# One attention and two-layer MLP kernel: GpSimd makes V's low part, and its planner gets new numbers

## The chip, the cores and the metric

The kernel runs on 1 core of a Trainium2 chip. The metric is the device time of one execution in microseconds; less is better.

## The reference

Attention with a threshold, then two gated MLP layers, all in float32:

```python
scores = (q @ k.T) / sqrt(64)                       # 4 batches, 8 heads, 576 rows, 64 columns
scores = where(scores >= max(scores, -1) - tau, scores, -1e9)
attn = exp(scores - max(scores, -1));  attn /= sum(attn) + 1e-9
x = attn @ v                                        # to 2304 rows of 512
h = x @ w_in                                        # 512 -> 2048
x = (h * tanh(softplus(h))) @ w_out                 # layer 1: Mish
h = x @ w2_in
out = (h * clip(h + 3, 0, 6) / 6) @ w2_out          # layer 2: hard swish
```

## The kernel before, in words

Precision is kept by splitting: each operand of a large matmul becomes a float16 high part and a float16 low part (the rest), and three products are summed. The low part of V, `vl`, is V times a scale `vs`, less its high part `vh`; the pv matmul adds both parts.

The weights come as 64-bit words and are turned into float32 by integer steps (`one_conversion`, L912): maximum (L785), scale, expansion on ScalarE (L921), a shift by three or a product by eight in two halves (c2: L929 on GpSimd, L931 on VectorE), two merges on VectorE (L937, L942). The first layer's weights (w1i, w1o) are then split in two (L961, L729); the second layer's go through a Strassen-like scheme with seven products (`combined`, L972), as does y between the layers (`split_sums`, L1100).

There are four stages. (1) Attention: for each of the 16 head pairs and each of 4 full query tiles and a tail tile of 64 rows, scores go to one of two PSUM buffers (`s`), VectorE takes the row maximum (`pk`, L1858), ScalarE the exponential (`ex`, L1868) and the threshold (`th`, L1863), VectorE the mask (`mk`, e_ex L1871), ScalarE the float16 high part (`ph`, L1876), GpSimd the low part (`pl`, L729 p_ph), a DMA transposes (`tr`), and PE multiplies with V (`pv`, L1897). (2) Woven into it, the first gemm of layer 1 for blocks of 256 rows whose attention is done (`inner`, L1260). (3) Layer 1's second gemm (`first_layer`, L1304), beside the conversion of w2i and w2o. (4) Layer 2, block by block (`second_layer`, L1381).

No order is written out by hand. Everything is a task with one or more engines, a duration for each (`{"dve": 0.88}`), buffers it holds, and a due time. `Plan.run` (L631) plays the tasks through a clock of each engine: again and again it takes for each engine the best candidate by due time among those that could start within a window (WINDOW, NEAR_LATE) and issues the one that starts first. This happens when the program is built; on the chip each engine works off its own list in order and waits on semaphores. So a duration in the code changes only the order, and, where a task names several engines (WHO, SHIFT, TAKE), who does it. A VectorE candidate for such a task is put back by SLOW in that comparison. The kinds in PORT are not planned beside GpSimd's.

Due times in the attention are START plus multiples of STEP; each task's own is shifted by NUDGE[name], and by EASE per kind. `V`'s loads and maxima are planned in `batch_values` (L1702), K's scaling, `vh` and `vl` in `pair` (L1748):

Of the kernel before, what the change touches and what calls it, by code (L numbers as in the profile page):

```python
# [52 lines left out]
PREP_AHEAD = 5.76
CONV_STEP = 1
CONV_AT = 5.423
LATE_STEP = 3.76
OUT_STEP = 2.681
OUT_AT = 149.789
V_AHEAD = 4.749
# [2167 lines left out]
```

## Time and profile before

| | us |
|---|---|
| median of 3 runs | 986.13 (984.49 to 987.72) |
| the profiled execution | 984.73 |
| its span, first to last instruction | 982.9 |
| PE busy | 922.2 (94%) |
| DVE busy | 797.9 (81%) |
| ACT busy | 650.8 (66%) |
| POOL busy | 409.2 (42%) |

PE is TensorE, DVE VectorE, ACT ScalarE, POOL GpSimd, SP SyncE, which issues the DMAs. The shares are means over stages with different limits, so they are to be read by stretches of the span.

### The profile page before, as it was taken

Reading aid. Unit: us, or ns where it says so; the run is one execution under the profiler, and the core shown is the slowest. Engines: PE = TensorE matmul, PEld = TensorE weight load, DVE = VectorE, ACT = ScalarE, POOL = GpSimd, SP = SyncE. Lnnn points to the kernel's source line nnn. Section 1 sums busy time; section 2 is a strip of 40 time slices with the busy share of each in tenths; the row PEclk is TensorE's granted clock in tenths of the full one; section 3 lists DMA queues with packets and bytes.
Section 4 is the critical chain, followed back from the end, with each engine's and each line's share of the span. In section 5 each row is a group of like instructions: output and inputs, shape, how many; then the busy total and the mean of one; then the engine's idle time right before and its main releaser. Section 6 shows DMA issues by size and latency. Waiting matters only on the chain.

```text
span 982.9 us, 25896 instructions
## 1 busy us (share of the span) xinstructions
PE 922.2 (94%) x10776; PEld 797.2 (81%) x10776; DVE 797.9 (81%) x1516; ACT 650.8 (66%) x1051; POOL 409.2 (42%) x354
## 2 busy tenths in 40 slices
PE   3669779999999999999999999999999999999996
PEld 1447457777777778888888888899999999999986
DVE  6998898888878888569999889888758758758864
ACT  6678688888888877567866778655444444545541
POOL 2777776766655667315656777720000000000000
PEclk9769789999999999999999999999999999999999
DMA  9899999999999999864654757750110110110001
GB/s 313 179 233 234 228 226 218 251 253 217 238 217 270 216 220 238 234 239 173 239 211 176 282 188 287 246 219 9 60 47 16 60 41 22 60 32 31 23 15 31
DMA packets 201798, 164.48 MB, mean 167 GB/s; under 512 B 174160, under 2 KB 174928, under 8 KB 195280
## 3 DMA queue, kind: packets, MB, share of 16 engines
q1 hardware_dynamic: 201680, 162.82, 61.1%
q8 instruction: 85, 1.39, 0.6%
q14 instruction: 33, 0.27, 0.1%
HBM read 84.28 MB, written 36.04 MB: 122 GB/s over the span
## 4 chain that ended last, share of the span: by engine, by line
PE 76%; DVE 13%; POOL 3%; DMA 3%; issue 2%; ACT 1%; SPq 0%; DVEq 0%; POOLq 0%; ACTq 0%
PE h_g L1241 15%; PE y_y L1356 13%; PE s_s L1849 7%; PE aux_pv L1897 5%; PE hp_g1a L1430 5%; PE h_g0a L1430 5%; PE hp_g1d L1430 2%; PE h_g0d L1430 2%; DMA pt_tr<-p_ph 2%; DVE e_ex L1871 2%; DVE nm_pk L1858 1%; POOL p_ph L729 1%; DVE top L785 1%; PE h_g1b L1430 1%; DVE gs_h L1336 1%
## 5 line engine op out<-in xcount | busy, mean ns | idle before, releaser
L729 POOL TENSOR_TENSOR p_ph<-e_ex,p_ph 128x128 f16<-128x128 f32 (+3 forms) x160 | 192.5, 1225 | 106.4 <-issue 54.8
L1583 PEld LDWEIGHTS <-gs_h 128*128 128x128 f16 x1512 | 146.8, 98 | 18.0 <-issue 1.5
L1430 PEld LDWEIGHTS <-w__h 128*128 128x128 f16 x2016 | 156.0, 98 | 1.2 <-issue 0.6
L1871 DVE SCALAR_TENSOR_TENSOR e_ex<-s_s,thr_th,e_ex 128x576 f32<-128x576 f32 x144 | 111.9, 812 | 15.3 <-ACT thr_th L1863 11.8
L1858 DVE TENSOR_REDUCE nm_pk<-s_s 128x1 f32<-128x576 f32 x144 | 104.6, 751 | 18.0 <-PE s_s L1849 17.0
L1868 ACT ACTIVATE e_ex<-s_s,nm_pk 128x576 f32<-128x576 f32 x144 | 104.1, 730 | 18.5 <-DVE nm_pk L1858 13.9
L1849 PE MATMUL s_s<-kd_lk,qs_qp 64*128 64x288 f32 x440 | 80.8, 480 | 36.4 <-DVE e_ex L1871 25.6
L1876 ACT ACTIVATE p_ph<-e_ex 128x576 f16<-128x576 f32 x144 | 94.8, 678 | 13.5 <-DVE e_ex L1871 9.1
L1430 PEld LDWEIGHTS <-w__u 128*128 128x128 f16 x1008 | 98.6, 98 | 0.0
L1897 PEld LDWEIGHTS <-pt_tr 128*128 128x128 f16 x2016 | 81.3, 103 | 11.1 <-issue 5.8
L1849 PEld LDWEIGHTS s_s<-kd_lk,qs_qp 64*128 64x128 f32 x440 | 41.4, 204 | 59.0 <-issue 39.5
L1897 PE MATMUL aux_pv<-vh,pt_tr 128*128 128x65 f16 (+1 forms) x1296 | 86.1, 203 | 1.9 <-DMA pt_tr<-p_ph 1.9
L729 DVE TENSOR_TENSOR gs_h<-g_ab,gs_h 128x896 f16<-128x896 f32 x72 | 74.6, 1087 | 15.9 <-ACT gs_h L1533 15.9
L1533 ACT ACTIVATE gs_h<-g_ab 128x1792 f16<-128x1792 f32 x36 | 59.6, 1690 | 27.4 <-DVE g_ab L729 27.4
L1897 PE MATMUL aux_pv<-vl_vl,pt_tr 128*128 128x64 f16 x720 | 70.7, 203 | 0.0
L1517 ACT ACTIVATE g_ab<-g_ab,aux,hscales 128x512 f32<-128x512 f32 x72 | 54.1, 804 | 16.9 <-DVE g_ab L1458 16.9
L1327 ACT ACTIVATE hp_e<-hl_l 128x512 f32<-128x512 f32 x72 | 42.4, 594 | 23.5 <-DVE gs_h L1336 23.2
L1290 ACT ACTIVATE he_t<-h_g,hin 128x512 f32<-128x512 f32 x63 | 42.9, 683 | 19.0 <-PE h_g L1241 15.1
L1523 DVE SCALAR_TENSOR_TENSOR g_ab<-g_ab,f 128x512 f32<-128x512 f32 x72 | 51.2, 747 | 5.0 <-ACT g_ab L1517 5.0
L1336 DVE SCALAR_TENSOR_TENSOR gs_h<-hp_e,fscales,gs_h 128x512 f16<-128x512 f32 x72 | 53.0, 743 | 2.1 <-ACT gs_h L1330 2.1
L1330 ACT ACTIVATE gs_h<-hp_e,fscales 128x512 f16<-128x512 f32 x72 | 47.3, 678 | 7.6 <-PE y_y L1356 6.8
L1448 ACT ACTIVATE s_ka<-h_g0a 128x512 f32<-128x512 f32 x27 | 16.1, 595 | 48.1 <-PE h_g0a L1430 47.9
(672 smaller groups left out, 2559.2 us busy)
## 6 DMA issues: line engine op xcount, KB each, us to landing
hd<-he_t SPq DMA_DIRECT2D x36, 512.0 KB, 4.2
hl_l<-hd SPq DMA_DIRECT2D x18, 1024.0 KB, 5.7
raw_lr<-in_moe_w_in SPq DMA_DIRECT2D x16, 1024.0 KB, 6.0
raw_lr<-in_moe_w_out SPq DMA_DIRECT2D x16, 1024.0 KB, 7.5
yd<-yl_zhy SPq DMA_DIRECT2D x9, 896.0 KB, 3.8
qs_qp<-in_q SPq DMA_DIRECT2D x10, 576.0 KB, 5.8
v_lv<-in_v SPq DMA_DIRECT2D x16, 320.0 KB, 4.7
kd_lk<-in_k SPq DMA_DIRECT2D x15, 288.0 KB, 3.9
```

The lines of the kernel that those rows point to most:

```text
L729: engine[e].tensor_tensor(dst, a, b, ALU.subtract)
L1241: mm(hv[:, j, :], wj[:, wl, c * P : (c + 1) * P], x.tile[:, c, xl, :], start=j == 0 and n == 0, stop=j == 1 and n == 11, skip_group_check= ...
L1336: nc.vector.scalar_tensor_tensor(s.tile[:, k, 1], g.tile.rearrange("p (a n) -> p a n", a=2), fs[:, fp : fp + 1], s.tile[:, k, 0], ALU.mult ...
L1356: mm(yv[:, h, :], wt[1][f // 2].tile[:, f % 2, wl, c * P : (c + 1) * P], gs[fp // COL].tile[:, fp % COL, gl, f % 2, :], start=fp == 0 and ...
L1430: mm(dst.tile[:, i * Q : (i + 1) * Q], wt[2][fp][wl].tile[:, right - 1, c * P : (c + 1) * P], x[xl].tile[:, c, left - 1], start=first and ...
L1583: mm(region(p), part[:, gl, left - 1], wt[3][fp][wl].tile[:, right - 1], start=fp == n == 0 and spot(p)[1] == 0, stop=fp == NG - 1 and n == 2,
L1849: mm(s[j].tile[:, half, :HALF], lh[r], rh[r], start=m == 0, stop=m == len(terms) - 1,)
L1858: nc.vector.tensor_reduce(neg.tile[:, j : j + 1], sv(j), AX.XY, ALU.max, negate=True)
L1868: nc.scalar.activation(ev(j), sv(j), AF.Exp, bias=neg.tile[:, j : j + 1])
L1871: nc.vector.scalar_tensor_tensor(ev(j), sv(j), thr.tile[:, j : j + 1], ev(j), ALU.is_ge, ALU.mult)
L1876: nc.scalar.activation(p16.tile[:, js, :S], e_.tile[:, js], AF.Copy)
L1897: mm(ov[:, dst, :d], pt.tile[:, j, ch, :], part.tile[:, src, vc, :], start=i == j == ch == 0 and part is vh, stop=j == w - 1 and ch == 8, ...
```

## The change

V's low part leaves VectorE. In `pair` both ways of making it are already there, and WHO["vl"] decides: before, one instruction `v_lo` on VectorE (scale and subtract); after, two on GpSimd, `v_scaled` (V times `vs`, in place) and `v_rest` (less `vh`), the second after the first, both due when the pair begins. Other entries of WHO let c2 of w2i's and w2o's conversions, their sums and low parts, y's low part and K's scaling go to other engines.

The planner's clock for VectorE, ScalarE and GpSimd now lets an instruction begin a little before the one ahead of it ends (OVERLAP), some thirty durations are new, and the constants and shifts (STEP, START, NUDGE and others) are new throughout: 2149 shifts stand where 1595 stood, 594 of these with the same value. No other operation is added or removed.

```diff
-STEP = 2.791
-START = 12
+STEP = 2.764
+START = 10.202
...
-V_FIRST = -0.435
+V_FIRST = 0.446
...
-SHIFT = {"pool": 1.0, "dve": 0.6}
+SHIFT = {"pool": 1.05, "dve": 0.43}
...
-SLOW = 0.413
+SLOW = 0.499
 WHO = {
-    "c20": ("dve",), "c21": ("pool",), "c30": ("pool", "dve"), "c31": ("pool", "dve"),
-    "q2": ("pool",), "q3": ("pool", "dve"), "u20": ("dve",), "u21": ("pool",),
-    "u30": ("pool",), "u31": ("pool", "dve"), "uy0": ("pool", "dve"), "uy1": ("dve",),
-    "kh": ("act",), "vh": ("act",), "vl": ("dve",), "q": ("dve",), "o0": ("dve",), "o1": ("dve",),
+    "c20": ("pool", "dve"), "c21": ("dve",), "c30": ("dve",), "c31": ("dve",),
+    "q2": ("pool", "dve"), "q3": ("pool", "dve"), "u20": ("pool",), "u21": ("pool", "dve"),
+    "u30": ("pool",), "u31": ("pool",), "uy0": ("dve",), "uy1": ("pool",),
+    "kh": ("pool", "act"), "vh": ("act",), "vl": ("pool", "dve"), "q": ("dve",), "o0": ("dve",), "o1": ("dve",),
 }
...
+OVERLAP = {"dve": 0.08, "act": 0.1, "pool": 0.04}
 NUDGE = {
...
             end = start + cost
-            self.clock[e] = end
+            self.clock[e] = max(start, end - OVERLAP.get(e, 0.0))
...
-        return task({"dve": 1.3}, top, [loaded], [raw], "zw" + name)
+        return task({"dve": 1.212}, top, [loaded], [raw], "zw" + name)
...
-        a = task({"dve": 1.28}, c3, b, [raw, t], "c" + nm)
-        a = task({"dve": 1.28}, c4, [a], [raw, t], "c" + nm)
+        a = task({"dve": 1.22}, c3, b, [raw, t], "c" + nm)
+        a = task({"dve": 1.22}, c4, [a], [raw, t], "c" + nm)
...
-                a = go({"act": 0.69}, relu, done, [g], f"r{fp}")
+                a = go({"act": 0.803}, relu, done, [g], f"r{fp}")
...
-                cost = {"dve": 0.17 + size / 960.0, "pool": 0.1 + size / 450.0}
+                cost = {"dve": 0.17 + size / 960.0, "pool": 0.2 + size / 490.0}
```

## Rows read from the trace of the kernel before

**Rows 1.** Page, head: span, PE's busy us (share) and instructions, granted clock in tenths.
```profile
span 982.9 us, 25896 instructions
...
PE 922.2 (94%) x10776; PEld 797.2 (81%) x10776; DVE 797.9 (81%) x1516; ACT 650.8 (66%) x1051; POOL 409.2 (42%) x354
...
PEclk9769789999999999999999999999999999999999
```

**Rows 2.** Stretch, length; busy us: PE, PEld, DVE, ACT, POOL; clock, DMA share, GB/s.
```profile
0.00:13.00 13.00, 2.66 (x8) 1.09 (x9) 6.28 (x15) 4.65 (x8) 1.52 (x16) 1.00 0.80 277
13.00:30.00 17.00, 10.50 (x71) 6.29 (x72) 15.79 (x34) 14.96 (x28) 7.90 (x7) 1.00 1.07 316
30.00:100.00 70.00, 52.51 (x557) 39.24 (x553) 65.29 (x137) 52.94 (x92) 54.18 (x50) 0.78 0.89 211
100.00:140.50 40.50, 27.93 (x266) 19.07 (x268) 34.56 (x79) 29.42 (x54) 27.16 (x25) 0.79 1.02 240
140.50:412.00 271.50, 269.23 (x3280) 213.52 (x3278) 230.82 (x427) 219.22 (x409) 174.16 (x157) 1.00 1.04 229
412.00:642.00 230.00, 227.73 (x2116) 203.94 (x2114) 201.11 (x344) 168.16 (x250) 142.20 (x101) 1.00 0.63 230
642.00:973.00 331.00, 329.30 (x4470) 312.28 (x4470) 240.99 (x480) 160.95 (x214) 2.12 (x2) 1.00 0.14 47
```

**Rows 3.** Waits of PE before 140.5 us: total us, times, longest us.
```profile
PE s_s L1849 <- DVE e_ex L1871: 27.8, 12, 4.7
```

**Rows 4.** Chain that ended last, 940 to 983 us: start us, us, what.
```profile
973.36 0.48 ACT out_v L1623
```

**Rows 5.** DVE's busy time of V's low part (L1799) alone, by stretches.
```profile
13.00:30.00 17.00, 2.55 (x3) 1.00 1.07 316
30.00:100.00 70.00, 1.36 (x1) 0.78 0.89 211
100.00:140.50 40.50, 0.97 (x2) 0.79 1.02 240
```

**Rows 6.** Chain that ended last, 0 to 32 us.
```profile
18.30 1.59 DVE vl_vl L1799 x2
...
23.22 2.30 PE s_s L1849 x8
```

**Rows 7.** POOL by form, whole run: operation, shape, count | busy us, mean ns | idle before.
```profile
L729 POOL TENSOR_TENSOR p_ph<-e_ex,p_ph 128x1024 f16<-128x1024 f32 x64 | 137.4, 2147 | 0.0
...
L729 POOL TENSOR_TENSOR p_ph<-e_ex,p_ph 128x512 f16<-128x512 f32 x16 | 18.6, 1160 | 0.0
...
L929 POOL TENSOR_TENSOR cvt_c__1_450<-cvt_c__1_450,eight 128x512 int32<-128x512 int32 x2 | 2.0, 1040 | 0.1
```

**Rows 8.** DVE by form, 0 to 150 us.
```profile
L1799 DVE SCALAR_TENSOR_TENSOR vl_vl<-v_lv,vs_ve,vh 128x640 f16<-128x640 f32 x7 | 6.7, 975 | 0.0
...
L937 DVE SCALAR_TENSOR_TENSOR cvt_c__1_841<-raw_lr,cvt_c__1_841 128x1024 uint32<-128x1024 uint32 x1 | 2.0, 2009 | 0.0
...
L937 DVE SCALAR_TENSOR_TENSOR cvt_c__1_975<-raw_lr,cvt_c__1_975 128x1024 uint32<-128x1024 uint32 x1 | 1.2, 1215 | 0.0
```

**Rows 9.** Groups by line, whole run.
```profile
L1871 DVE SCALAR_TENSOR_TENSOR e_ex<-s_s,thr_th,e_ex 128x576 f32<-128x576 f32 x144 | 111.9, 812 | 15.3 <-ACT thr_th L1863 11.8 <-ACT e_ex L1868 2.9
...
L1517 ACT ACTIVATE g_ab<-g_ab,aux,hscales 128x512 f32<-128x512 f32 x72 | 54.1, 804 | 16.9 <-DVE g_ab L1458 16.9
...
L785 DVE TENSOR_REDUCE top<-raw_lr 128x1 f32<-128x1024 f32 x32 | 38.8, 1212 | 5.3 <-DMA raw_lr<-in_moe_w_in 3.1 <-DMA raw_lr<-in_moe_w_out 2.1
```

**Rows 10.** Timeline, 0 to 32 us: start us, us, instruction, count [idle before <-releaser].
```profile
8.26 2.49 DVE L1713 TENSOR_REDUCE vt_vm<-v_lv 128x1 f32<-128x640 f32 x3 [0.81 <-DMA v_lv<-in_v]
...
10.66 0.75 DVE L1858 TENSOR_REDUCE nm_pk<-s_s 128x1 f32<-128x576 f32 x1
...
12.05 1.53 DVE L1871 SCALAR_TENSOR_TENSOR e_ex<-s_s,thr_th,e_ex 128x576 f32<-128x576 f32 x2
```

More of the change, by code (lines that the diff above doesn't have):

```diff
@@ L46 @@
 RELEASE = dict.fromkeys(("s", "m", "h", "y", "aux"), 0.27)
-STEP = 2.791
-START = 12
-PV_OFF = 3.422
-V_FIRST = -0.435
+STEP = 2.764
+START = 10.202
+PV_OFF = 3.416
+V_FIRST = 0.446
 FIRST_AHEAD = 3
[L53 to L59, printed above, removed]
+PREP_AHEAD = 5.912
+CONV_STEP = 1.133
+CONV_AT = 5.509
+LATE_STEP = 1.5
+OUT_STEP = 5.008
+OUT_AT = 130.543
+V_AHEAD = 4.287
 MOE_OFF = 9.75
-MOE_LAG = 13.595
+MOE_LAG = 14.145
 RATE = 0.9
 NX = 3
-FLIP = 3.348
-ALPHA = {"act": 7.907, "pe": 3.022}
-FITS = 0.015
+FLIP = 2.882
+ALPHA = {"act": 9.47, "pe": 1.987}
+FITS = 0.219
 PORT = ("vl", "c", "u", "o", "zs", "q", "p")
@@ L72 @@
 MERGE_LO = True
-SHIFT = {"pool": 1.0, "dve": 0.6}
-TAKE = {"act": 0.6, "dve": 0.74}
+SHIFT = {"pool": 1.05, "dve": 0.43}
+TAKE = {"act": 0.687, "dve": 0.75}
 EVAC = {"act": 0.6}
-NORM_TAIL = {"dve": 0.39, "act": 0.43}
+NORM_TAIL = {"dve": 0.39, "act": 0.62}
 VECTOR = 0.17
@@ L97 @@
 PARTS = 4
-JOIN = 2.448
-JOIN_FROM = 340.468
-STAY = 0.954
+JOIN = 1.182
+JOIN_FROM = 324.517
+STAY = 0.771
 NBLK_EARLY = 2 * B - 2
+OVERLAP = {"dve": 0.08, "act": 0.1, "pool": 0.04}
 NUDGE = {
[323 rows of a table removed]
[438 rows of a table added]
 }
-EASE = {"mk": -6, "ph": 2.117, "pl": 0.391, "tr": 1.5, "ex": 2.281, "s": -5.48, "th": -2.308}
+EASE = {"mk": -3.967, "ph": 1.256, "pl": 0.409, "tr": 0.792, "ex": 2.288, "s": -6, "th": -2.834}
 P_LO = ("pool",)
-EXPAND = {"act": 1.15}
+EXPAND = {"act": 1.24}
 BUFS = {"e": 4, "p16": 4}
 LATE = {"gs": 2, "hl": 2, "h": 2, "y": 2}
-WINDOW = {"pe": 0.17, "dve": 0.095, "act": 0.232, "pool": 0.789, "sp": 0}
-PAD = {"zp": 0.834, "zpy": 0.374, "zps": 1.772}
-NEAR_LATE = {"pe": 0, "dve": 0.087, "act": 0, "pool": 0.606, "sp": 0.21}
-OFF_LATE = 6.941
-OFF_FINAL = 29.238
-LATE_AT = 11.587
-OFF_SECOND = 40
+WINDOW = {"pe": 0.184, "dve": 0.095, "act": 0.264, "pool": 0.725, "sp": 0.13}
+PAD = {"zp": 0.53, "zpy": 0.314, "zps": 3}
+NEAR_LATE = {"pe": 0, "dve": 0.07, "act": 0.045, "pool": 0.556, "sp": 0.21}
+OFF_LATE = 8.641
+OFF_FINAL = 28.039
+LATE_AT = 12.199
+OFF_SECOND = 39.183
 class Ring:
@@ L968, in one_conversion @@
             converted[m, 2 * g + j] = task(
-                {"pool": 1.25, "dve": 0.68}, lambda e, j=j: lo(e, j), [a], [t, dst], f"u{nm}{j}"
+                {"pool": 1.18, "dve": 0.68}, lambda e, j=j: lo(e, j), [a], [t, dst], f"u{nm}{j}"
             )
@@ L1016, in combined @@
                 task(
-                    pick(f"u{m}{x}", pool=0.1 + size / 450, dve=0.1 + size / 960),
+                    pick(f"u{m}{x}", pool=0.1 + size / 490, dve=0.1 + size / 960),
                     lambda e, x=x: lo(e, x),
@@ L1091, in go @@
         def go(fn, deps, n):
-            cost = pick(who, pool=0.74, dve=0.4)
+            cost = pick(who, pool=0.74, dve=0.42)
             return task(cost, fn, deps, bufs, f"q{name}_{n}")
@@ L1120, in lo @@
             sub(e, dst.tile[:, 1, c], xf.tile[:, c, 1:], dst.tile[:, 0, c])
-        a = task({"act": 1.37}, take, [a], [src, xf, sm], "zv" + name)
+        a = task({"act": 1.262}, take, [a], [src, xf, sm], "zv" + name)
         def quarter(j, t):
@@ L1139, in split_sums @@
         for n, fn in enumerate((differ, add_right(5, 6), last, add_right(4, 0))):
-            a = task({"dve": 0.4}, fn, [a], [src, xf, sm], f"v{name}_{n}")
+            a = task({"dve": 0.477}, fn, [a], [src, xf, sm], f"v{name}_{n}")
         made = [a]
@@ L1144, in split_sums @@
             task(
-                pick(f"uy{c}", pool=2.3, dve=1.2), lambda e, c=c: lo(e, c), [a], [xf, dst],
+                pick(f"uy{c}", pool=2.3, dve=1.1), lambda e, c=c: lo(e, c), [a], [xf, dst],
                 f"u{name}_{c}",
@@ L1229, in link @@
             chain[name] = task(
-                {"pe": 0.109 * piece + 0.01}, lambda e, i=i: fn(i, i + piece), deps, bufs,
+                {"pe": 0.1092 * piece}, lambda e, i=i: fn(i, i + piece), deps, bufs,
                 f"{tag}{i}", 0.0, unit, [chain[name]],
@@ L1342, in first_layer @@
             a = chain["gs"] = task(
-                {"act": 0.63}, hi, [a, scaled], [g, s], f"h{fp}", 0.0, fp, [chain["gs"]]
+                {"act": 0.682}, hi, [a, scaled], [g, s], f"h{fp}", 0.0, fp, [chain["gs"]]
             )
@@ L1439, in product @@
                 chain["g1"] = task(
-                    {"pe": 0.0563 * 6 * COL}, mms, [*loaded, *weights, *deps], [dst, *held],
+                    {"pe": 0.0559 * 6 * COL}, mms, [*loaded, *weights, *deps], [dst, *held],
                     f"g{u}{tag}", 0.0, u, [chain["g1"]],
@@ L1450, in copy @@
                         nc.vector.tensor_copy(kept.tile[:, k], src.tile)
-                return task({"act": 0.65, "dve": 0.66}, copy, deps, [src, kept], f"k{tag}{u}", 0.0, u)
+                return task({"act": 0.6, "dve": 0.69}, copy, deps, [src, kept], f"k{tag}{u}", 0.0, u)
             def plus(src, k, slot, deps, tag):
@@ L1461, in go @@
                         )
-                return task({"dve": 0.86}, go, deps, [src, kept, *pairs], f"a{tag}{u}", 0.0, u)
+                return task({"dve": 0.757}, go, deps, [src, kept, *pairs], f"a{tag}{u}", 0.0, u)
             def straight(src, slot, deps):
@@ L1472, in copy @@
                             nc.vector.tensor_copy(*args)
-                return task({"act": 0.85, "dve": 0.84}, copy, deps, [src, *pairs], f"k{u}", 0.0, u)
+                return task({"act": 0.66, "dve": 0.757}, copy, deps, [src, *pairs], f"k{u}", 0.0, u)
             p1 = product(X, 1, 2, True, [], "a")
@@ L1478, in unit @@
                 a = task(
-                    {"dve": 0.16}, scales, [y_stored[blk], scaled_by["y"]], [], "zx", 0.0, 0, [p1]
+                    {"dve": 0.27}, scales, [y_stored[blk], scaled_by["y"]], [], "zx", 0.0, 0, [p1]
                 )
@@ L1541, in finish @@
                     go(
-                        pick(f"o{k}", pool=2.35, dve=1.2), lambda e, k=k: lo(e, k), [a], [g, part],
+                        pick(f"o{k}", pool=2.5, dve=1.087), lambda e, k=k: lo(e, k), [a], [g, part],
                         f"o{first}_{k}",
@@ L1611, in factor_out @@
             nc.vector.tensor_scalar(xs(blk, 1), xs(blk, 0), const_y[:, 1:2], None, ALU.mult)
-        factored = task({"dve": 0.15}, factor_out, [*scaled, scaled_by["out"]], [], "zo", 0.0, NG - 1)
+        factored = task({"dve": 0.21}, factor_out, [*scaled, scaled_by["out"]], [], "zo", 0.0, NG - 1)
         side_, yo = Buf(r_out), Buf(r_out)
@@ L1631, in step @@
             return task(
-                {"dve": 0.42}, go, [ready[n], *deps], [*of(n), side_, yo], f"v{tag}", 0.0, NG
+                {"dve": 0.477}, go, [ready[n], *deps], [*of(n), side_, yo], f"v{tag}", 0.0, NG
             )
@@ L1642, in store @@
             task({"sp": 0.6}, go, deps, [yo], tag, 0.4 * len(halves), NG)
-        s1 = task({"act": 0.42}, seed, [ready[0], factored], [*of(0), side_], "v", 0.0, NG)
+        s1 = task({"act": 0.475}, seed, [ready[0], factored], [*of(0), side_], "v", 0.0, NG)
         u2 = step(lambda: temp(1), 5, lambda: temp(0), [s1], "a")
@@ L1788, in pair @@
             lq += [prev[4]] * w
-            cost = pick("kh", act=0.14 + 0.29 * w, pool=0.07 + 0.83 * w)
+            cost = pick("kh", act=0.19 + 0.29 * w, pool=0.07 + 0.83 * w)
             kl += [prep(cost, lambda e, js=js: k_scaled(e, js), [lk], [kd], "kh")] * w
@@ L1916, in query_tiles @@
                 exs.append(go({"act": 0.735}, lambda e, j=j: exp(j), [a], [s[j], neg, e_], "ex", j))
-            th = go({"act": 0.2}, threshold, pks, [neg, thr], "th")
+            th = go({"act": 0.295}, threshold, pks, [neg, thr], "th")
             mks = [
@@ L1946, in query_tiles @@
             a = go(
-                {"pe": 0.87 if c < NQ else 0.8}, pv, [a, prev[1], prev[3], split], [pt, o, vh, vl],
+                {"pe": 0.86 if c < NQ else 0.81}, pv, [a, prev[1], prev[3], split], [pt, o, vh, vl],
                 "pv", 0, 0.0, PV_OFF * STEP,
@@ L1988, in norm @@
                         nc.vector.tensor_scalar_mul(*args, weight)
-            a = add({"dve": 0.21}, total, [last, scaled], [o, vs, den], at, 0.0, 0.0, "dt" + nm)
+            a = add({"dve": 0.175}, total, [last, scaled], [o, vs, den], at, 0.0, 0.0, "dt" + nm)
             a = add({"dve": 0.17}, rec, [a], [den], at, 0.0, 0.0, "dr" + nm)
@@ L2145, in fused_kernel @@
     task = tasker(at)
-    scaled_by["y"] = task({"dve": 1.1}, second_scales, [scaled_by[i] for i in range(4)], [], "zy")
+    scaled_by["y"] = task({"dve": 2.0}, second_scales, [scaled_by[i] for i in range(4)], [], "zy")
     scaled_by["out"] = task({"dve": 0.3}, out_scale, [scaled_by["y"]], [], "zo")
```

4 lines of the change are left out of this document (2 added, 2 removed), and 761 rows, old and new, of the table NUDGE.

## The prediction

> **What bounds the kernel now.** I read the head of the page first: PE is busy 922 of 982.9 us, and the granted clock is below full only early [rows 1]. The busy time by stretches says where PE is not full [rows 2]. Before 140.5 us it is busy 2.66 + 10.50 + 52.51 + 27.93 = 93.6 us, so 46.9 us are idle, and from 30 to 140.5 us the granted clock is 0.78 to 0.79, a mix of its two levels (1.2 and 2.4 GHz), with PE idle for 30.1 of these 110.5 us. After that PE is idle only 271.5 - 269.2 = 2.3, 230 - 227.7 = 2.3 and 331 - 329.3 = 1.7 us up to 973 us: 6.3 us in 832. The reader is to see two kernels in one: until about 140 us another engine sets the pace, later PE does and nothing else matters.
>
> Which engine it is early, the same rows tell: from 13 to 140.5 us DVE is busy 15.79 + 65.29 + 34.56 = 115.6 of 127.5 us (91%), ACT 97.3 (76%), POOL 89.2 (70%). The waits agree: of the PE idle time before 140.5 us the largest part, 27.8 us, is scores waiting for the mask on DVE (e_ex, L1871) to give a PSUM buffer back [rows 3]. DVE does the attention's row maxima and masks and, at once, the conversion of w1i. After the last matmul, at 973.36 us, a chain of ACT, DVE and stores follows [rows 4]; nothing in the change alters its instructions.
>
> So the question is how far the change moves the point from which PE is full. One us won there is one us of the whole, as everything behind it is a row of PE work of fixed length.
>
> **The change, part by part.** The sum is made against the profiled execution (984.7 us, 1.4 below the median of the three runs, 986.1).
>
> *V's low part leaves DVE.* Today it is one DVE instruction for each of 16 head pairs. By stretches they cost DVE 2.55 + 1.36 + 0.97 = 4.9 us before 140.5 us [rows 5]; the other 9.8 us lie where PE is full and are worth nothing. Two of the early ones stand in the chain itself: 1.59 us at 18.30, between a mask and the maxima, with the scores of 23.22 behind them [rows 6]. As DVE is the limit for 91% of the time, 4.9 x 0.91 = 4.4 us are won. Bounds: 0 if DVE gets as much other work back (below), 4.9 at most. I take 4.4, since the chain passes through it.
>
> *What GpSimd gets.* Two instructions over 128x640 per pair: a scaling of V in place and a subtraction. Neither is in the trace. The subtraction is nearest to p_ph: 1160 ns for 128x512 and 2147 for 128x1024, so about 1.41 us between them; the scaling is nearest to the one-operand integer step, 1040 ns for 128x512, so 1.30 us [rows 7]. 2.7 us a pair is the estimate; the plan's own prices (1.95 + 1.6 = 3.55) are the upper bound, twice the 512 row of the integer step (2.1) the lower. That is 43 us for 16 pairs (34 to 57). Four pairs fall before 100 us: 10.8 us (8.3 to 14.2) on a POOL that is busy 7.9 + 54.2 = 62.1 of 87 us, which gives 84% (81 to 88%). It fits on the mean, so I cost it at nothing; it is less roomy at the start, where three pairs (8.1 us) meet 9.1 us of idle POOL in 13 to 30 us. There the low parts of the probabilities, their transposes and pv stand behind V in POOL's queue; buffers of p16 and e four deep cover a few us. If that cover is gone, the price is the second rival's.
>
> A second cost is on DVE: conversion steps that run beside POOL can be held up. Such a step took 2009 ns at worst where its like took 1215, and V's own step averaged 975 ns in this stage [rows 8]. Six pairs fall before 140.5 us [rows 5], 16 us more on a POOL that is busy for 89; if hold-ups grow as POOL's time does, that is 0.18 of the 0.8 seen in the worst one, and I add twice that, 0.3 us; the upper bound is one such hold-up of 0.8 us for each of the twelve steps, 9.5 us, which is a rival (below). The Trainium skill's page "SBUF — State Buffer", section "Who interferes with whom", says that a DVE instruction with two SBUF inputs and a GpSimd instruction that reads SBUF exclude each other for a whole instruction; the held-up steps above agree with it. By that rule alone, every V step that starts beside such a DVE instruction would cost the bound and not the 0.3; the forecast goes by the row, which shows it for a few steps only.
>
> *New prices and overlap in the planner.* The planner issues nothing on the chip; it only settles each engine's order. Before, its durations were off: it charged relu 0.69 us and the maximum of a weight 1.3, while the trace has 804 and 1212 ns, and the new figures (0.803 and 1.212) are those [rows 9]. It let each DVE instruction begin when the last ended, while two masks that take 812 ns each by the page [rows 9] end 1.53 us after the first begins [rows 10], an overlap of 0.09, and the new OVERLAP for DVE is 0.08. With 250 DVE instructions in 13 to 140.5 us [rows 2] the old plan's DVE was up to 250 x 0.08 = 20 us late by 140 us, and an order made with a wrong clock makes queues wait for one another. What can be won is DVE's idle time there, 127.5 - 115.6 = 11.9 us. One such place is visible: the second head's maximum starts at 10.66, because three maxima of V (2.49 us) were put in front of it, and the first mask then waits for it [rows 10]. I take a third of the idle time, 4 us; bounds are all 11.9 and, on the other side, one more wait of the longest kind, 4.7 [rows 3], lost.
>
> *Everything from 140.5 to 973 us.* Another order cannot save more than PE's 6.3 us of idle, and may add as much; 0, with +-3. Here lie the choices for w2i, w2o and y (c2x, c3x to DVE, most u to POOL, uy swapped): up to 24 integer steps move to DVE, at most 24 x 1.04 = 25 us [rows 7] on a DVE with 230 - 201.1 = 28.9 us free [rows 2], under a PE that is 99% busy. K's scaling may go from ACT to POOL; ACT is not the limit early. Due times of loads on SP's queue move by a few us with START and STEP; nothing shows a queue that waits for SP there. All cost 0; if the cover in 412 to 642 us goes, it is a us or two per stop. The tail is 0.
>
> Sum: -4.4 + 0.3 - 4.0 = -8.1; 984.7 - 8.1 = 976.6. **Forecast 977 us.**
>
> **The rivals.** *First, a larger gain:* the new order wins all of DVE's idle time before 140 us: -4.4 - 11.9 = -16.3, 968 us. For it: the idle is spread over many short waits, which a plan with right durations can fill. Against: part of it waits for loads and for PE.
>
> *Second, slower: GpSimd's queue.* It runs in order. If the V pairs are put ahead of low parts of probabilities that are due, each holds them back 2.7 us, then the transposes and pv, and so the first block's x, which the first gemm1 needs. Four pairs before 100 us cost 10.8 us, less the 4.4 won on DVE: +6.4, 991 us. It decides as soon as POOL has no idle time between 13 and 30 us, which three pairs at the plan's own price (10.7 us against 9.1 of idle) would bring about. For it: this, and that conversions of w1i hang on POOL up to 100 us at 77%. Against: the buffers and the mean of 84%.
>
> *Third, no change:* DVE gets back what it gave. The planner may now hand w1i's integer steps to DVE (price cut from 0.6 to 0.43) when POOL is taken, and ten of them eat 4.3 us of the 4.4. Or each of the twelve V steps holds a DVE step up by the 0.8 us of the worst row [rows 8], and 9.5 us go against the 8.4 won. Either way 984 us. The Trainium skill's page named above has this rival's rule; the traces bear it out for single steps. That the V move does nothing at all would look the same.
>
> **How the numbers follow.** Forecast 0.50 (970 to 983), larger gain 0.13, no change 0.17, slower 0.20. About 0.3% (3 us) is what a measurement of this kernel can tell from no change. A little of the forecast's case falls within it: faster 0.61, same 0.19, slower 0.20. The range takes in the larger gain and most of the slower case: 965 to 990.
>
> **What would show it.** Right: no V low part on DVE, and 32 more POOL instructions in two forms of 128x640 near 1.3 and 1.4 us; PE full from about 132 us instead of 140.5; "scores wait for mask" before that point clearly under 27.8 us; from there to the last matmul the same 833 us. The first term is wrong if DVE has no less work in that stage, the second if its idle time there is still near 12 us. The forecast as a whole is wrong if the late stretch changes by more than 3 us, or if POOL's V steps take over 2 us each and pv waits for them.

## The result, and the profile after

The changed kernel is slower: 993.41 us, median of 6 runs (990.26 to 995.23), beside 986.92 us (984.49 to 990.22) for the kernel before on the same chip; ratio 1.0058 (95% interval 1.0033 to 1.0083). The forecast was 977 us, with a range of 965 to 990. The profiled execution took 990.26 us, with this head of its page:

```profile
span 988.5 us, 25942 instructions
...
PE 925.0 (94%) x10776; PEld 799.9 (81%) x10776; DVE 789.8 (80%) x1518; ACT 645.1 (65%) x1038; POOL 457.7 (46%) x381
...
PEclk9777979999999999999999999999999999999999
```

The work moved as the diff says: DVE has 8 us less than in [rows 1], POOL 48.5 us more. Yet the span is 5.6 us longer. The busy time by stretches (columns as in [rows 2]) tells where:

```profile
13.00:30.00 17.00, 8.71 (x36) 4.31 (x37) 15.10 (x33) 14.94 (x26) 13.93 (x11) 1.00 1.01 288
30.00:100.00 70.00, 49.53 (x531) 36.36 (x528) 61.95 (x127) 48.69 (x86) 60.15 (x52) 0.73 0.88 194
100.00:140.50 40.50, 29.33 (x303) 21.49 (x300) 34.23 (x82) 31.70 (x59) 33.43 (x29) 0.85 1.07 249
140.50:412.00 271.50, 267.74 (x3255) 212.55 (x3256) 227.90 (x423) 214.94 (x399) 205.37 (x178) 1.00 1.04 229
412.00:642.00 230.00, 226.93 (x2071) 202.47 (x2069) 194.66 (x348) 168.95 (x250) 134.50 (x95) 0.99 0.66 235
642.00:973.00 331.00, 331.00 (x4511) 314.15 (x4510) 244.98 (x488) 159.81 (x213) 8.84 (x4) 1.00 0.13 46
```

Behind 412 us PE is as full as before. Ahead of it PE lost: 49.53 instead of 52.51 us in 30 to 100, at a granted clock of 0.73 instead of 0.78, a mix of the levels 1.2 and 2.4 GHz [rows 2]. And PE is not yet full at 140.5 us. The same view of 140.5 to 156 us, before and then after:

```profile
140.50:156.00 15.50, 15.50 (x192) 12.15 (x189) 14.66 (x26) 12.48 (x24) 10.92 (x9) 1.00 0.91 211
```
```profile
140.50:156.00 15.50, 12.32 (x150) 9.29 (x150) 14.33 (x23) 11.84 (x21) 12.23 (x10) 0.95 0.85 233
```

What PE has done less is the first gemm of layer 1, gemm1 for short. Its line alone in 0 to 150 us (PE, PEld, clock, DMA share, GB/s), before and after:

```profile
0.00:150.00 150.00, 30.36 (x225) 22.09 (x226) 0.84 0.94 236
```
```profile
0.00:150.00 150.00, 20.78 (x168) 15.59 (x168) 0.83 0.94 229
```

That is 57 matmuls fewer; they start 0.109 us apart where they follow one another, so 6.2 us of PE's work, about the 5.6 us of the span. (Over all of PE's matmuls it is 57 fewer as well, 962 instead of 1019.) I use this count, "gemm1 matmuls by 150 us", for every run below. The first of them comes 10 us later (first and last start of the group on the first weights, before and after):

```profile
L1241 PE MATMUL h_g<-x_fl,w__h__1_540 x192: 270/273/418, 74.6 to 407.5; 128*128 128x256 f16 x192
```
```profile
L1357 PE MATMUL h_g<-x_fl,w__h__1_541 x192: 271/273/283, 84.6 to 412.4; 128*128 128x256 f16 x192
```

The late start is mostly made up by 125 us: the count is 64 instead of 120 by 100 us and 144 instead of 158 by 125 us. Then a new gap opens, to 168 instead of 225 by 150 us. In 125 to 153 us PE's listed waits are 5.3 us before and 9.6 us after. The largest after (total us, times, longest):

```profile
PE s_s L1965 <- DVE e_ex L1987: 4.9, 3, 2.8
PE aux_pv L2013 <- DMA pt_tr<-p_ph: 2.6, 1, 2.6
PE aux_fl L2127 <- DVE xn_dn L2090: 1.7, 1, 1.7
```

Where did DVE's freed time go? Busy time in 13 to 153 us (PE, PEld, DVE, ACT, POOL, ...), before and after:

```profile
13.00:153.00 140.00, 103.44 (x1048) 74.59 (x1049) 127.43 (x264) 106.89 (x189) 99.04 (x88) 0.83 0.95 232
```
```profile
13.00:153.00 140.00, 96.90 (x989) 69.36 (x990) 123.29 (x257) 104.21 (x184) 117.28 (x99) 0.82 0.95 224
```

V took 6.7 us of DVE [rows 8]; DVE is busy 4.1 us less, so 4.1 us of these turned into idle time: 12.6 us before, 16.7 after. DVE's waits in that stretch (total us, times, longest), before and after:

```profile
DVE nm_pk L1858 <- PE s_s L1849: 4.5, 9, 1.0
DVE top L785 <- DMA raw_lr<-in_moe_w_in: 3.1, 3, 1.5
DVE cvt_c__1_1405 L937 <- POOL cvt_c__1_1405 L929: 1.7, 1, 1.7
```
```profile
DVE e_ex L1987 <- ACT thr_th L1979: 4.6, 7, 1.1
DVE top L901 <- DMA raw_lr<-in_moe_w_in: 3.2, 4, 1.2
DVE nm_pk L1974 <- PE s_s L1965: 2.0, 6, 0.7
```

The maxima wait less for scores, but masks now wait 4.6 us for ACT's threshold; in this stretch the trace of before has no such wait. PE's wait for masks before 140.5 us fell from 27.8 us [rows 3] to 22.1 (24.9 by 155 us, as PE is full later); a wait for the transposed probabilities took its place:

```profile
PE s_s L1965 <- DVE e_ex L1987: 22.1, 13, 4.8
...
PE aux_pv L2013 <- DMA pt_tr<-p_ph: 4.9, 3, 2.6
```

And this is what V costs POOL, 0 to 150 us by form:

```profile
L1926 POOL TENSOR_SCALAR v_lv<-v_lv,vs_ve 128x640 f32<-128x640 f32 x7 | 13.2, 1891 | 0.1
...
L845 POOL TENSOR_TENSOR vl_vl<-v_lv,vh 128x640 f16<-128x640 f32 x7 | 9.5, 1357 | 0.2
```

### The profile page after: what moved, and what is told of

It is laid out like the page before. It is cut to its first block, busy times and chain, and to the rows that moved or that the text cites. A ratio compares the mean times of both kernels' runs of the same rounds, so it can differ in the third digit from the quotient of the medians.

```text
span 988.5 us, 25942 instructions
## 1 busy us (share of the span) xinstructions
PE 925.0 (94%) x10776; PEld 799.9 (81%) x10776; DVE 789.8 (80%) x1518; ACT 645.1 (65%) x1038; POOL 457.7 (46%) x381
## 4 chain that ended last, share of the span: by engine, by line
PE 79%; DVE 9%; DMA 5%; ACT 2%; issue 2%; POOL 1%; SPq 1%; DVEq 0%; ACTq 0%; POOLq 0%
PE h_g L1357 17%; PE y_y L1472 14%; PE s_s L1965 8%; PE aux_pv L2013 6%; PE hp_g1a L1546 5%; PE h_g0a L1546 5%; PE hp_g1d L1546 2%; PE h_g0d L1546 2%; DMA pt_tr<-p_ph 2%; DVE e_ex L1987 2%; DMA raw_lr<-in_moe_w_in 2%; PE h_g1b L1546 1%; PE hp_g0b L1546 1%; DMA v_lv<-in_v 1%; PE y_y__1_8_0_15100 L1699 1%
## 5 line engine op out<-in xcount | busy, mean ns | idle before, releaser
L1965 PE MATMUL s_s<-kd_lk,qs_qp 64*128 64x288 f32 x520 | 96.0, 486 | 33.2 <-DVE e_ex L1987 21.4
L1965 PEld LDWEIGHTS s_s<-kd_lk,qs_qp 64*128 64x128 f32 x520 | 50.1, 208 | 62.1 <-issue 41.4
L1443 ACT ACTIVATE hp_e<-hl_l 128x512 f32<-128x512 f32 x72 | 42.4, 595 | 28.6 <-DVE gs_h L1452 27.0
L1406 ACT ACTIVATE he_t<-h_g,hin 128x512 f32<-128x512 f32 x56 | 38.3, 685 | 20.0 <-PE h_g L1357 18.4
```

Source lines behind the costliest of these rows:

```text
L1965: mm(s[j].tile[:, half, :HALF], lh[r], rh[r], start=m == 0, stop=m == len(terms) - 1,)
```

## The experiments

The change has two halves: V's low part on GpSimd, and a new order. They can be taken apart, because the kernel's planner only yields a list of steps for each engine (4127 steps before, 4143 after). In the runs named "fixed order" that list was written into the kernel and issued as it is, so that nothing moves but what the diff names. Ratios are to the kernel before, run beside it.

### V and the order taken apart

*V to GpSimd in the fixed order of before.*

```diff
-"vl": ("dve",)
+"vl": ("pool",)    # two steps, at the old step's place in GpSimd's order
```

> The order of the kernel before, kept instruction by instruction on every engine (it is read from a list instead of being searched for); only V's low part leaves VectorE for two GpSimd instructions at the same place. If V on GpSimd is what costs (theory 1: its queue holds up the probabilities), this is slower than before by 4 us or more, 990 to 995. If the new order is what costs (theory 2), this is within 3 us of before, or faster by up to the 4.4 us that the forecast's first term promised, 982 to 987.

Measured 999.75 us, 1.0131 (1.0107 to 1.0154). This is above even theory 1's range.

*V back to DVE in the fixed order of after.*

```diff
-"vl": ("pool", "dve")
+"vl": ("dve",)     # one step, where GpSimd's first step stood
```

> The changed kernel's order, kept instruction by instruction; only V's low part goes back to one VectorE instruction, at the place of the first of the two GpSimd steps. Theory 1 (V on GpSimd costs): back to the time of before or better, 983 to 988. Theory 2 (the order costs): still 991 to 996, and up to 4 us above the changed kernel, since VectorE gets 0.9 us a pair back.

Measured 1000.73 us, 1.0139 (1.0119 to 1.0159): 7 us above after, and above theory 2's range too. Each order fits its own engine for V and loses with the other one. The two runs together settle neither theory, since both edits put work where the order had kept no room for it.

*V's steps emptied, in either order.* V's low part is left out, the order stays.

```diff
-nc.gpsimd.tensor_scalar(vb.tile, vb.tile, vs.tile, None, ALU.mult)
+one = vb.tile[:, :1, :1, :1]
+nc.gpsimd.tensor_scalar(one, one, vs.tile, None, ALU.mult)
...
-sub("pool", vl.tile, vb.tile, vh.tile[:, :, :, :D])
+nc.gpsimd.memset(vl.tile, 0.0)
```

> The changed kernel and its order; V's low part is left out: its two GpSimd steps are a one-column scaling and a fill with zeros, some 0.4 us a pair instead of 3.25. Theory 1: at least 5 us below the changed kernel, 988 or less. Theory 2: within 2 us of it, 991 to 994.

Measured 992.49 us, 1.0055 (1.0037 to 1.0074), the ratio of after itself; 162 matmuls by 150 us, as against 168.

```diff
-nc.vector.scalar_tensor_tensor(vl.tile, vb.tile, vs.tile, vh.tile[:, :, :, :D], ALU.mult, ALU.subtract)
+nc.vector.memset(vl.tile, 0.0)
```

> The kernel before and its order; V's low part is left out: its VectorE instruction is a fill with zeros, some 0.2 us instead of 0.92. This is the forecast's first term by itself: if VectorE's time in the first 140 us is the path, 3 to 4 us below before (983). If something else sets the pace there, within 1 us of before.

Measured 985.56 us, 0.9987 (0.9971 to 1.0003). The emptied steps are short, not gone: a pair takes GpSimd 0.91 us instead of 3.25, and DVE's seven fills by 150 us take 2.3 us instead of 6.7:

```profile
L1799 DVE MEMSET vl_vl<- 128x320 uint32 x7 | 2.3, 325 | 0.1
```

So V's steps, on whichever engine, are worth about one us in their own order, and with most of V's work gone from both the orders still differ by 992.5 - 985.6 = 6.9 us. **The loss is the new order's; the time that V's steps take on GpSimd is not the reason.** One rival stays: the new order was made around V on GpSimd. The planner kept 3.55 us a pair there and puts no PORT kind beside it; emptying the steps gives the time back, not the places. No run has the new constants planned with V on DVE, so whether the order is worse because it had to make room for V is open. DVE's busy time in 13 to 153 us (columns as above) shows why so little came of it, first in the order of before with V emptied, then in the order of after:

```profile
13.00:153.00 140.00, 102.49 (x1020) 74.16 (x1022) 121.73 (x262) 106.44 (x188) 95.75 (x86) 0.82 0.95 229
```
```profile
13.00:153.00 140.00, 95.78 (x950) 68.14 (x950) 121.08 (x250) 101.58 (x180) 98.09 (x96) 0.82 0.91 217
```

In the first, DVE has 5.7 us less work and 5.7 us more idle time (127.43 to 121.73), and PE is no better off. The maxima now wait 6.6 us for scores, as against 4.5 before:

```profile
DVE nm_pk L1856 <- PE s_s L1847: 6.6, 14, 1.0
```

### What a microsecond of DVE is worth

*V's low part computed twice on DVE.*

```diff
 nc.vector.scalar_tensor_tensor(vl.tile, vb.tile, vs.tile, vh.tile[:, :, :, :D], ALU.mult, ALU.subtract)
+nc.vector.scalar_tensor_tensor(vl.tile, vb.tile, vs.tile, vh.tile[:, :, :, :D], ALU.mult, ALU.subtract)
```

> The kernel before with V's low part computed twice on VectorE (the same instruction, issued again): seven more of 0.98 us before 150 us, 6.8 us, and nine later. Theory D (one us of VectorE's time before 140 us is one us of the whole, as the forecast had it): 991 to 994 us. Theory G (V's steps mostly fill time in which VectorE waits for others; taking all of them away gave 1.3 us): 986.5 to 989.

Measured 1001.86 us, 1.0162 (1.0141 to 1.0184): 15 us, above both theories. The copies took DVE 21.5 us in all, 7.7 of these ahead of 150 us, and not the 0.98 us each that was expected: three that were queued beside low parts on GpSimd took 2.6 us. The copies by 150 us, by form:

```profile
L1802 DVE SCALAR_TENSOR_TENSOR vl_vl<-v_lv,vs_ve,vh 128x640 f16<-128x640 f32 x5 | 7.7, 1542 | 0.2
```

So this edit adds collisions too. The gemm1 matmuls by 150 us fell from 225 to 172, which is 5.8 us. The rest was lost behind 150 us, where PE had been nearly full (PE, clock, DMA share, GB/s; before, then with the copies):

```profile
150.00:412.00 262.00, 259.73 (x3158) 1.00 1.05 230
```
```profile
150.00:412.00 262.00, 255.49 (x3054) 0.99 1.05 223
```

*w1i's two merges on half the columns.*

```diff
-t.tile, high(raw), 0x80000000, t.tile, ALU.bitwise_and, ALU.bitwise_or
+t.tile[:, :1], high(raw)[:, :1], 0x80000000, t.tile[:, :1], ALU.bitwise_and, ALU.bitwise_or
```

> The kernel before with VectorE's two merges of every group of w1i done on half of the columns only (this leaves out half of that conversion): 16 instructions of 1.22 us become about 0.62, 9.6 us less of VectorE before 141 us, and each group's chain of conversion is 1.2 us shorter. Theory D (VectorE's time is the path at one to one): 977 to 981 us. Theory G (what is freed turns into waiting): 984 to 987.

Measured 983.05 us, 0.9960 (0.9945 to 0.9975): 3.8 us, and 238 matmuls by 150 us. The sixteen merges took 12.6 us instead of 20.9, so 8.4 us less and not 9.6; they also shorten the chain of each group, so this is not DVE's time alone. The time lies between both theories. The mechanism is G's: the maxima's wait for scores rose from 4.5 to 7.8 us.

Taking DVE's work away wins 0.3 (1.3 of 4.4) to 0.45 (3.8 of 8.4) of it, adding it costs 0.7 of all that is added (15 of 21.5 us). By the intervals of the ratios the first two can be up to 0.65, and the last is at least 0.65. So to add is likely dearer than to take away, but these runs only just tell the two apart; a price of 0.91, as forecast, is none of them. A reading that fits: in a given order a delay is handed on to every queue that waits, and time that comes free is only used where the next step's other inputs are early too.

### Where in the new order

*The order of before until 170 us of the plan, then that of after, and the reverse* (fixed orders; each step keeps the place of its source).

```diff
+order = [s for s in before if s.start < 170]
+order += [s for s in after if s not in order]
```

> The order of before until 170 us of the plan, and from there the order of after (pairs 0 to 7 have V's low part on VectorE as before, pairs 8 to 15 on GpSimd as after). Theory E (the new order loses in the first 170 us, where gemm1 of block 0 waits for the weights w1i): 984 to 988 us, about the kernel before, give or take the seam. Rival L (the new order loses later, for instance at the wait of 2.9 us near 541 us): 990 to 995.

Measured 992.26 us, 1.0055 (1.0038 to 1.0071). By time this is rival L's, but its trace says otherwise: 221 matmuls by 150 us, like before, and then a loss at the seam. In 150 to 200 us, where PE was full before, it now waits for masks (windows, PE first; 160 to 180 us):

```profile
160.00:170.00 10.00, 6.71 (x80) 4.79 (x77) 7.02 (x13) 6.14 (x12) 6.16 (x6) 0.83 0.86 155
170.00:180.00 10.00, 9.26 (x100) 6.84 (x100) 9.33 (x18) 7.39 (x14) 5.59 (x5) 0.83 0.70 153
```

Probably the rest of the new order counts on its own state at 170 us, which the old order doesn't leave behind; no run tests that.

> The mirror image: the order of after until 170 us of the plan, with V's low part on GpSimd for the pairs begun by then, and from there the order of before. Theory E (the loss is in the first 170 us): 991 to 996 us. Rival L (the loss is later): 984 to 988.

Measured 995.25 us, 1.0084 (1.0067 to 1.0101), as theory E has it: 168 matmuls by 150 us, exactly after's count. Its own seam costs little: from 150 to 200 us PE is busy 48.9 of 50 us, as against 49.2 in after. Over the profiles, five runs with the new order's beginning (after, this one, a_v_empty, a_threshold, a_pool_gap) stand at 159 to 168 by 150 us, six with the old one's (before, b_v_empty, hy_ba170, hy_ba420 and the two runs with a thousandth, below) at 196 to 231. So the loss comes with the first 150 us of the new order.

*The order of before until 420 us, then that of after* (V on DVE throughout).

> The order of before until 420 us of the plan, where the attention is over, and from there the order of after; V's low part on VectorE throughout. Under a clock with the overlaps and the new durations this order takes 985.1 us and before's 991.3. Theory C (the new order is better late, as that clock says): 979 to 983 us, faster than both kernels. Rival (TensorE is full there in either order; work done by TensorE up to each time differed by under 3 us after 430 us): 985 to 990.

Measured 987.08 us, 0.9993 (0.9975 to 1.0012): the same as before. Late, neither order is better.

### Candidates for the step that costs it

*w1i's conversion first.* Fixed order of after, groups 2 to 7 (then 4 to 7 alone) ahead where their inputs allow:

```diff
-DVE, by the plan: ... merges of group 4 (98.4 and 104.5 us) ... merges of group 6 (129.8 and 133.5) ...
+DVE, ACT, POOL: w1i's steps up to 15 us (12 us) ahead, the others in their old order
```

> The order of after, with the steps that convert w1i's groups 2 to 7 put up to 15 us ahead on each engine where their inputs allow, and gemm1 of block 0 and the attention steps in their old order around them; by the kernel's own plan the low part of the last group ends at 144.5 us instead of 151.3. Theory W (the conversion of w1i paces TensorE until about 150 us, so the 6 us come back): 985 to 989 us, and TensorE full from about 145 us instead of 153. Rival A (the attention steps that are pushed back cost as much): 991 to 997.

> The order of after with the conversion of w1i's groups 4 to 7 alone put up to 12 us ahead where its inputs allow (the run that moved groups 2 to 7 also pushed block 0's attention back, and so its first gemm1 by 12 us); by the plan the last group ends at 145.0 us instead of 151.3, and the first gemm1 stays. Theory W (the last groups of w1i pace TensorE between 114 and 153 us): 985 to 989 us. Rival A (the attention steps that they pass cost as much or more): 991 to 998.

Measured 1006.03 us, 1.0192 (1.0170 to 1.0214), and 1007.38, 1.0215 (1.0198 to 1.0233). Theory W would have these faster. But neither edit was clean: in both the first matmul of gemm1 came at 96.8 us or later, as the steps let loose also passed block 0's attention. So they show only that more haste for the weights costs more than it brings here.

*Thresholds ahead of weight expansions on ACT* (fixed order of after).

```diff
-ACT: ... expansion of a group (1.25 us), threshold ...
+ACT: ... threshold, expansion of a group (1.25 us) ...     # five places
```

> The order of after with five thresholds of ScalarE before 155 us put ahead of the weight expansion (1.25 us) that they stand behind; nothing else moves. In the trace of after VectorE's mask waits 4.6 us in seven places for the threshold, in the trace of before nowhere. Theory T (this wait is where VectorE's freed time went, and it is on the path): 988.5 to 991 us. Rival (the expansion is as urgent, or the wait is off the path): 992.5 to 996.

Measured 995.82 us, 1.0084 (1.0062 to 1.0106); 161 matmuls by 150 us. DVE's waits in 13 to 153 us:

```profile
DVE top L994 <- DMA raw_lr<-in_moe_w_in: 6.1, 3, 4.3
DVE e_ex L2080 <- ACT e_ex L2077: 3.9, 5, 1.0
DVE e_ex L2080 <- ACT thr_th L2072: 2.9, 5, 0.7
```

The threshold's wait fell by 1.7 us, but a wait for the exponential took its place, and the one for weights grew. Over both steps of ACT the mask waited 6.8 us instead of 5.3. So moving the thresholds did not take the wait away, and what after would take without it is not shown.

*Ready probabilities into GpSimd's gap* (fixed order of after).

```diff
 POOL: ... integer steps of w1i's group 1 (to 39.8 us)
+POOL: low parts of two tiles of probabilities
 POOL: low part of w1i's group 0 (44.3 us, after a wait of 4.6)
...
-POOL: low parts of two tiles of probabilities (47.7 us)
```

> The order of after with one pair's two low parts of the probabilities on GpSimd (ready at 33 and 40 us, done at 50 and 53) put ahead of the weights' low part for which GpSimd waits 4.6 us at 39.7 to 44.3 us; nothing else moves. Theory Q (GpSimd's queue holds up block 0's probabilities, and with them the first gemm1, which came at 84.6 us instead of 74.6): 988 to 991 us, first gemm1 before 81 us. Rival (other steps are as late): 992 to 994, first gemm1 at 84 to 85 us.

Measured 995.85 us, 1.0094 (1.0069 to 1.0118); first gemm1 at 85.8 us. Theory Q's gain did not come, and the trace gives a reason that I had not seen: in the gap DVE ran w1i's four merges, whose result GpSimd's next step needs, and the planner keeps the two engines apart there (PORT). So the edit also delayed the merges, and does not settle what an earlier low part alone would win. GpSimd and DVE in 38 to 50 us, by form:

```profile
L938 POOL TENSOR_TENSOR p_ph<-e_ex,p_ph 128x1024 f16<-128x1024 f32 x2 | 6.2, 3098 | 0.0
L938 POOL TENSOR_TENSOR p_ph<-e_ex,p_ph 128x128 f16<-128x128 f32 x2 | 2.8, 1406 | 0.0
```
```profile
L1151 DVE SCALAR_TENSOR_TENSOR cvt_c__1_324<-raw_lr,cvt_c__1_324 128x1024 uint32<-128x1024 uint32 x1 | 3.1, 3140 | 0.0
...
L1146 DVE SCALAR_TENSOR_TENSOR cvt_c__1_324<-raw_lr,cvt_c__1_324 128x1024 uint32<-128x1024 uint32 x1 | 1.6, 1572 | 0.0
L1146 DVE SCALAR_TENSOR_TENSOR cvt_c__1_486<-raw_lr,cvt_c__1_486 128x1024 uint32<-128x1024 uint32 x1 | 1.4, 1444 | 0.0
L1151 DVE SCALAR_TENSOR_TENSOR cvt_c__1_486<-raw_lr,cvt_c__1_486 128x1024 uint32<-128x1024 uint32 x1 | 1.4, 1444 | 0.0
```

and the same four merges in after, with GpSimd idle beside most of them:

```profile
L1053 DVE SCALAR_TENSOR_TENSOR cvt_c__1_324<-raw_lr,cvt_c__1_324 128x1024 uint32<-128x1024 uint32 x1 | 1.7, 1694 | 0.0
L1058 DVE SCALAR_TENSOR_TENSOR cvt_c__1_324<-raw_lr,cvt_c__1_324 128x1024 uint32<-128x1024 uint32 x1 | 1.2, 1210 | 0.0
L1058 DVE SCALAR_TENSOR_TENSOR cvt_c__1_486<-raw_lr,cvt_c__1_486 128x1024 uint32<-128x1024 uint32 x1 | 1.2, 1210 | 0.0
L1053 DVE SCALAR_TENSOR_TENSOR cvt_c__1_486<-raw_lr,cvt_c__1_486 128x1024 uint32<-128x1024 uint32 x1 | 1.2, 1209 | 0.0
```

Side by side the four take 7.6 us instead of 5.3, and a 128x1024 low part 3.1 instead of 2.15 [rows 7]. The Trainium skill's page "SBUF — State Buffer", section "Who interferes with whom", says that a DVE instruction with two SBUF inputs and a GpSimd instruction that reads SBUF exclude each other for a whole instruction. This run agrees: the low part that began at 41.3 us ended 2.0 us after the merge ahead of it (at 42.4), and the merge that began at 42.3 ended 1.1 us after that low part (at 44.4). Each waited for the other and then took about its own time, which makes 3.1 us for both.

### The planner's clock alone

*Before, planned anew with the overlaps only; then with the overlaps and the new durations.* V stays on DVE, all due times and corrections stay.

```diff
-self.clock[e] = end
+self.clock[e] = max(start, end - OVERLAP.get(e, 0.0))
...
-return task({"dve": 1.3}, top, [loaded], [raw], "zw" + name)     # second run only, as the other durations
+return task({"dve": 1.212}, top, [loaded], [raw], "zw" + name)
```

> The kernel before, planned anew with one thing changed: the plan's clock lets instructions of one engine overlap at their ends (0.08, 0.1 and 0.04 us on VectorE, ScalarE and GpSimd). V's low part stays on VectorE, and the durations, due times and corrections stay the old ones. The forecast's second term (the right clock finds idle time that the old one hid): 981 to 985 us. Rival (the chip lets them overlap whatever the plan says, so that the new plan is only another order): 986 to 997.

> The kernel before planned anew with the overlaps in the plan's clock and with the new durations, and nothing else: V's low part stays on VectorE, due times, windows and corrections stay the old ones. The forecast's second term by itself: 982 to 985 us. Rival R (a plan made anew loses what the old order had, whatever its clock says): 990 to 1005. The plan's own length falls by 8.4 us, from 1001.4 to 993.0.

Measured 1003.24 us, 1.0167 (1.0148 to 1.0187), and 1004.15, 1.0181 (1.0155 to 1.0207). Neither gains; both lose 17 us. But due times and corrections in them were fitted to the old clock, and much of the loss lies elsewhere than after's: the gemm1 count by 150 us is 168 and 176, and from 412 to 642 us PE is busy only 221.2 and 220.6 of 230 us (227.7 before, 226.9 after). So they do not show what the corrected clock does with the new constants.

*Before's order with w1i's conversion and gemm1's first matmuls let loose under the corrected clock, everything else fixed* (the diff is as for a_w1i_early, in the order of before).

> The order of before, with the steps of w1i's conversion and gemm1's first matmuls free to go as soon as a plan clock with the overlaps and the new durations finds them ready, everything else in its old order (some 50 instructions on VectorE, ScalarE and GpSimd and 516 matmul rows change place). That clock gives before's order 991.3 us and this one 987.2. Theory C (what the corrected clock gains, the chip gains): 981 to 984 us. Rival (the chip's gains and losses of an order are not those of that clock): 986 to 995.

Measured 995.19 us, 1.0084 (1.0070 to 1.0098). The beginning is no better (215 matmuls), and its profile has one new stop of PE late, where a load now comes too late:

```profile
PE h_g0a L1635 <- DMA xl_x__1_0_0_9797<-yd: 5.5, 1, 5.5
```

*Before, planned anew with one duration changed by a thousandth,* as a measure of what any new plan costs.

```diff
-return task({"dve": 1.3}, top, [loaded], [raw], "zw" + name)
+return task({"dve": 1.301}, top, [loaded], [raw], "zw" + name)
```

> The kernel before planned anew with one duration changed by a thousandth: VectorE's maximum over a weight group is 1.301 us instead of 1.300. No theory of V or of the clock gives this any effect, and the forecast's way of counting gives 0. Rival R (an order not tuned again loses by itself): 990 to 1003; the plan's own length grows by 15.8 us, all of it after 160 us.

```diff
-a = add({"dve": 0.21}, total, [last, scaled], [o, vs, den], at, 0.0, 0.0, "dt" + nm)
+a = add({"dve": 0.211}, total, [last, scaled], [o, vs, den], at, 0.0, 0.0, "dt" + nm)
```

> As the run with one duration changed by a thousandth, with another one: VectorE's step that sums the denominators is 0.211 us in the plan instead of 0.210. The plan's own length changes by 0.6 us only, from 1001.4 to 1002.0. If a plan made anew loses by itself even where its clock sees nothing: 989 to 1000 us. If the loss of the first such run came only from what its clock saw (15.8 us longer): 986 to 988.

Measured 995.74 us, 1.0088 (1.0065 to 1.0112), for the first: a thousandth of a us in one price costs about as much as the whole change did (1.0058; the intervals overlap). For the second 988.14 us, 1.0012 (0.9996 to 1.0028), the same as before. So a new plan need not lose by being new. But both keep before's order on every engine until about 290 us, so neither tests what another order of the first 150 us costs: that before's beginning was simply a good one, and most others are worse, is not ruled out. The old clock told the two apart: 15.8 us longer by its count, and 0.6. Beside one another (length of the plan by its own clock, which is no time of the chip, and the median time):

| planned with | kernel | plan, us | median, us | median - plan |
|---|---|---|---|---|
| old clock | before | 1001.4 | 986.9 | -14.5 |
| old clock | a thousandth, second | 1002.0 | 988.1 | -13.9 |
| old clock | a thousandth, first | 1017.2 | 995.7 | -21.5 |
| overlaps | b_overlap | 996.5 | 1003.2 | +6.7 |
| overlaps and durations | after | 985.0 | 993.4 | +8.4 |
| overlaps and durations | b_clock_durations | 993.0 | 1004.2 | +11.2 |

The old clock is 14 to 22 us too slow. It ranks its three plans as the chip does, though of the 15.8 us that it saw the chip shows 8.9. Plans made with the corrected one come out 6.7 to 11.2 us later than they say, and its other promises failed as well: against before's 991.3 us by that clock it gave hy_ba420 985.1 and b_free_w1i 987.2, and on the chip the first is the same as before and the second 8 us slower. It looks as if the 0.08 us that the old clock left between DVE's instructions were a margin for what no clock here knows (merges of 1.2 us that take 2 or 3), and plans without it hand every such delay on. That reading is argued from six plans; no run put a margin back into the new one.

## Why the prediction was wrong

**What bounds the kernel: right in place, wrong in kind.** As the prediction said, the difference lies ahead of the point from which PE is full, and behind it nothing changed: PE is idle 230 - 226.9 = 3.1 and 0 us in the last two stretches, 4.0 before [rows 2]. That point moved to about 153 us, not to 132. The first step that failed is "one us won there is one us of the whole" together with "DVE is the limit for 91% of the time". A busy share of 91% was read as a price of 0.91 per us. The runs show 0.3 to 0.45 for time taken away and 0.7 for time added. The 9% of waits in between were the sign: DVE's steps are one link of loops (scores, maximum, threshold, exponential, mask), and with V emptied the maxima waited longer for scores (6.6 us instead of 4.5). Nor is DVE's time behind 140 us worth nothing in both directions: with V computed twice PE lost 4.2 us of busy time in 150 to 412 us. One reading is off without weight: the last matmul ends at 975.3 us, not at 973.36.

**First term, V off DVE: -4.4 forecast, -1.3 measured** for the 4.4 us that b_v_empty takes away by 150 us (0.9987, with an interval that takes in 1). Mis-sized for that reason; even the two instructions in the chain of [rows 6] gave little.

**GpSimd's price: 2.7 us a pair forecast, 3.25 measured,** within the bounds of 2.1 to 3.55. The subtraction was right (1.41 and 1.36 us), the scaling was not: 1.30 taken from the integer step of [rows 7], 1.89 measured. That it costs nothing holds in the order that was made for it: a_v_empty has after's time. In the order of before, which has no room for it, it cost 13 us (b_on_pool).

**Hold-ups: +0.3.** The longest merges of w1i in 0 to 150 us take 2.32 and 1.86 us, as against 2.01 us for the longest in [rows 8]; the first of these ran beside V's own subtraction on GpSimd. All sixteen took 22.0 us instead of 20.9, so 1.0 us more where 0.3 was forecast; not what decides. a_pool_gap shows how real they are where work is put beside a merge.

**Second term, order and durations: -4.0 forecast.** This is the step that decided, and it has the wrong sign: with V emptied the new order is 6.9 us worse than the old one, while V off DVE and on GpSimd come to about -1.3 and +0.9, both small against the noise. The prediction took DVE's late clock in the plan for a fault on the chip. But nothing on the chip waits for the plan's clock: before's span of 982.9 us was already 18.5 us shorter than its plan. Replanned with the corrected clock and nothing else before lost 17 us. DVE's idle time, "what can be won", rose from 12.6 to 16.7 us in 13 to 153 us. Two of the signs that were to show the forecast right came true and meant nothing: no V on DVE, and scores that wait 22.1 instead of 27.8 us for the mask.

**Rivals.** The second (991 us, chance 0.20) came nearest in time, and its first sign came true: the first gemm1 was 10 us late. Its mechanism did not. GpSimd kept 3 us of idle time in 13 to 30 us, taking most of V's time away there won nothing (a_v_empty), and ready probabilities moved ahead won nothing (a_pool_gap). No rival had a new order that is simply worse. The nearest words were the lower bound of the second term, one wait of 4.7 us lost, which was put into the range and not into a case.

**Open.** Which steps of the new order's first 150 us cost the 6 us. Most of the gap opens after 125 us, where PE waits for masks, transposed probabilities and normalized rows. It is not the time that V's steps take. Thresholds, GpSimd's two tiles and w1i's place are not settled, as each of those edits moved a wait or delayed other steps. Nor is it settled whether making room for V on GpSimd shaped that order, or whether most other orders lose against before's. No run here beats the kernel before with the full computation.

## What to carry to other kernels

A busy share says how much an engine does, not what a microsecond of it is worth: take one step's work away and see whether the time falls or the engine idles. Measure that price in both directions, and read from the trace how long the added or emptied step really takes: here a copy expected at 0.98 us took up to 2.6, and an emptied step kept a third of its time. And a planner with the truer clock need not be the better planner; before its clock is mended, see whether its plans rank as the chip does, and plan once with a change that means nothing, as a null, and look from where on the order differs.
